# Decays a third phase ahead, and four pairs' x transposed by the DMA crossbar, in a fused recurrent-attention and MLP kernel

## Chip, cores, metric

One core of a Trainium2 chip. The metric is the device time of one execution in microseconds (us). A "run" below is one timed execution; every kernel has several, and the kernel before was timed beside each group of kernels on the same chip.

## The reference

Gated linear attention over 4 batches, 8 heads, 768 steps, heads of 48; its result, 3072 tokens of 384, goes through a GELU MLP of width 2048.

```python
for t in range(S):
    state = alpha[:, :, t, :, None] * state + einsum('bhd,bhe->bhde', k[:, :, t], v[:, :, t])
    y[:, :, t] = einsum('bhd,bhde->bhe', q[:, :, t], state)
x = y.transpose(0, 2, 1, 3).reshape(B * S, H * D)      # B, H, S, D = 4, 8, 768, 48
h = x @ w_in
g = 0.5 * h * (1 + tanh(sqrt(2 / pi) * (h + 0.044715 * h**3)))
out = g @ w_out
```

## The kernel before

Time is cut into 6 chunks of 128 steps; a **pair** is one chunk of two batches, so there are 12 pairs, 0 to 11. For each pair:

- the *decays*: `la` = ln(alpha) on ScalarE, its cumulative sum `cum` on TensorE, then `b`, `binv` and `bend` (exponentials) on ScalarE; VectorE makes `qp` = q·b and `kp` = k·binv;
- the transposes of qp and kp to `qkT`, by TensorE (through PSUM and a copy) or, for pairs 8 to 11, by the DMA crossbar;
- attention: `at` (scores), mask to `atm`, `kv` and the state, `y`;
- `x` is copied from `y` and transposed to `xT`: in this kernel always by TensorE through PSUM.

Each pair's tokens are then one **block** of the MLP: layer 1 (`hT`, 48 matmuls), GELU on ScalarE (`gT`), layer 2 (`acc`, 32 matmuls). A phase below is layer 1 and layer 2 of one block; the attention of later pairs is placed between these matmuls. ScalarE needs one table for ln and exp and another for GELU, so decays are done in stretches between the GELUs of two blocks:

```python
DECAYS = {-1: (0, 1), 1: (2, 3), 2: (4,), 3: (5,), 4: (6,), 5: (7,), 6: (8,), 7: (9,), 8: (10,), 9: (11,)}
TURN_QK, TURN_X = (8, 9, 10, 11), ()       # pairs whose qk, whose x go by the crossbar
```

Key 6 with value (8,) says: pair 8's decays come after block 6's GELUs. The rest is placed by a list scheduler that runs while the program is built, with an estimated duration for each task; it decides the order on every engine, and which of two engines does a copy. The two ways of transposing x, and what joins them:

```python
def turn_x_dma(self, u, i, c, b):
    return lambda e: self.nc.sync.dma_start_transpose(self.xT[c][:, :, b, :], u["x", i])
...
if m in self.TURN_X:
    xe = tx = s.add("turn", {"SP": W["turn"]}, P + 22 + j, self.turn_x_dma(u, j, c, b), [xc], xbar=W["xbar_x"])
else:
    tx = s.add("tx", {"PE": W["tx"]}, P + 22 + j, self.turn_x(u, j), [xc])
    xe = s.add("xe", {"DVE": W["xe"]}, P + 22 + j, self.turned_x(u, j, c, b), [tx])
```

All crossbar transposes and all stores of results are issued by SyncE, in one order. The loads of q, k, v and alpha are issued by GpSimd, but for the first of alpha.

Of the kernel before, what the change touches and what calls it, by code (L numbers as in the profile page):

```python
# [24 lines left out]
class Task:  # L25


    def __init__(self, kind, cost, prio, emit, deps=(), table=None, land=None, stream=None, xbar=0):
        self.kind, self.cost, self.prio, self.emit = kind, cost, prio, emit
        self.deps, self.takes = list(deps), []  # L30
        self.table, self.land, self.stream, self.xbar = table, land, stream, xbar
        self.end = self.done = None

    def take(self, tag, *users):
# [4 lines left out]
class Scheduler:  # L39
# [9 lines left out]
    def order(self):  # L49
        free = {e: 0 for e in LAT}  # L50
        taken = {tag: [] for tag in self.bufs}
        table, wire, xbar, head, out = LN_EXP, 0, 0, 0, []
        left = {e: sorted((t for t in self.tasks if e in t.cost), key=lambda t: t.prio) for e in LAT}

        def given(tag):

            n, at = len(taken[tag]) - self.bufs[tag], 0
            for u in taken[tag][n] if n >= 0 else ():
                if u.done is None:
                    return None  # L60
                at = max(at, u.done)
            return at

        def ready(t):
            if t.stream not in (None, head):
                return None
            at = 0
            for d in t.deps:
                if d.done is None:
                    return None  # L70
                at = max(at, d.done)
            for tag, _ in t.takes:
                g = given(tag)
                if g is None:
                    return None
                at = max(at, g)
            return at

        def put(t, at, e):
            nonlocal wire, xbar  # L80
            for tag, users in t.takes:
                taken[tag].append(users)
            t.start, t.end, t.engine, t.load = at, at + t.cost[e], e, None
            free[e] = t.end
            t.done = t.end + LAT[e]
            if t.land is not None:
                wire = t.done = max(wire, t.end + W["dma"] - t.land) + t.land
            if t.kind in ("turn", "store"):
                xbar = t.done = max(xbar, t.end + W["landed"] - t.xbar) + t.xbar
            out.append(t)  # L90

        while any(left.values()):
            best = None
            for e in LAT:
                found = []
                for t in left[e]:
                    at = ready(t)
                    if at is not None:
                        turn = W["table"] if t.table not in (None, table) else 0
                        at = max(at, free[e] + turn)  # L100
                        found.append((at, t, at - turn))
                if found:
                    window = min(f[2] for f in found) + 60
                    at, t, _ = min((f for f in found if f[2] <= window), key=lambda f: (f[1].prio, f[0]))
                    if best is None or at < best[0]:
                        best = at, e, t
            assert best is not None, "no task can go on"
            at, e, t = best
            if e == "PE" and self.fill and at < self.until and at - free[e] > 500:
                g = given("ff")  # L110
                n = int((at - max(free[e], g if g is not None else at) - 100) * 0.8 // W["fill"])
                if not free[e]:
                    n = int((at - W["zero"]) // W["cold"])
                if n > 0:
                    f = Task("fill", {"PE": n * W["fill"]}, 0, self.fill(n))
                    put(f.take("ff", f), max(free[e], g), e)
            put(t, at, e)
            if t.stream is not None:
                head += 1
            if t.table not in (None, table):  # L120
                table = t.load = t.table
            for q in t.cost:
                left[q].remove(t)
        return out
# [9 lines left out]
class _Kernel:  # L134

    BLOCKS = ((0,), (1,), (2,), (3,), (4,), (5,), (6,), (7,), (8,), (9,), (10,), (11,))
    DECAYS = {-1: (0, 1), 1: (2, 3), 2: (4,), 3: (5,), 4: (6,), 5: (7,), 6: (8,), 7: (9,), 8: (10,), 9: (11,)}

    SPLIT = (2,)
    EARLY = (0, 1)  # L140
    LOADS = ("0", "1", "in 0", "in 1", "in 2", "in 3", "out 0", "out 1", "out 2", "out 3",
             "2", "3", "4", "5", "6", "7", "8", "9", "10", "11")

    TURN_QK, TURN_X = (8, 9, 10, 11), ()
    BUFS = dict(ca=1, yk=2, ff=4, la=3, qp=3, kp=3, b8=2, qkT=3, atm=6, x=3, ot=6, bend=6,
                a=4, q=4, k=4, v=6)

    def __init__(self, ctx, tc, q, k, v, alpha, w_in, w_out, out):
# [24 lines left out]
                      for b in range(B)]  # L173
        self.ring = {n: [const.tile([C, 2, H, 64], F16 if n == "la" else BF16, name=f"{n}{i}")
                         for i in range(self.BUFS[n])] for n in ("la", "qp", "kp")}
        self.used = {n: 0 for n in self.ring}
# [5 lines left out]
    def tile(self, tag, shape, dt, name=None):  # L182
        pool = self.ps if tag in ("ca", "yk", "ff") else self.sb
        return pool.tile(shape, dt, tag=tag, bufs=self.BUFS[tag], name=name or tag)

# [73 lines left out]
    def exp(self, u, n, lo, hi):  # L259
        D, H = self.D, self.H  # L260

        def emit(e):
# [4 lines left out]
            else:  # L267
                if n not in u:
                    u[n] = self.sb.tile([self.C, 2, H, D], BF16, tag=n, bufs=self.BUFS["b8"], name=n)
                self.nc.scalar.activation(u[n].rearrange("t i h d -> t i (h d)")[:, lo:hi],  # L270
# [156 lines left out]
    def tasks(self):  # L427
        s = self.s = Scheduler(self.BUFS, self.fill, 60000)
        B, NCH = self.B, self.NCH
# [115 lines left out]
        f, gs, l2s = {}, {}, {}  # L545
        between = {m: [x for p in self.DECAYS.get(m, ()) for x in ends[p]] for m in range(-1, len(self.BLOCKS))}

# [15 lines left out]
        def layer2(m):  # L563
            nonlocal n
            units = [(pairs[p][0], 2 * pairs[p][1] + j) for p in self.BLOCKS[m] for j in range(2)]
            parts = range(self.NFT // 4)
            first = {}
            for u, part in ([(u, part) for part in parts for u in units] if m == 0 else [(u, part) for u in units for part in parts]):
                c, b = u
                t = s.add("l2", {"PE": W["l2"]}, 10000 + n, self.layer2(f, c, b, part),  # L570
                          gs[m][4 * part:4 * part + 4] + [loads["w", "out", part]], stream=n)
                l2s.setdefault(c, []).append(t)
                n += 1
                first.setdefault(u, t)
                if part == parts[-1]:
                    ot = s.add("ot", {"DVE": W["ot"], "ACT": W["ot_act"]}, -1, self.result(f, c, b), [t])
                    first[u].take("ff", ot)
                    ot.take("ot", s.add("store", {"SP": W["sp"]}, n, self.store(f, c, b), [ot]))

        for m in range(len(self.BLOCKS)):  # L580
            layer1(m)
            if m:
                for j in (0, 1) if m == 1 else (m,):
                    layer2(j)
        for m, ps in self.DECAYS.items():
            for p in ps if m >= 0 else ():
# [3 lines left out]
    def run(self):  # L590
# [5 lines left out]
        first = [lambda: make_upper_triangular(nc, self.ut_h, val=1.0, diag=True), lambda: make_identity(nc, self.ident)]  # L596
        for i in range(max(self.BUFS[n] for n in self.ring)):
            for n in self.ring:
                if i < self.BUFS[n]:
                    nc.vector.memset(self.ring[n][i][:, :, :, self.D:64], 0.0)  # L600
# [42 lines left out]
```

## Time and profile before

| | |
|---|---|
| time, median of 3 (range) | 190.5 us (190.08 to 190.57) |
| span of the profiled run; its time | 188.2 us; 190.31 us |
| TensorE, VectorE, ScalarE busy | 94%, 58%, 71% |
| table loads on ScalarE | 20 of 1.28 us |
| start of the last `ot` copy (the end of all matmuls) | 184.53 us |

How long the crossbar took for q and k, from the view of the tile qkT (time of the issue on SyncE, min/median/max in ns, start of the first and the last in us; then the time from issue to landing, of q and k together):

```profile
L308 SPq DMA_TRANSPOSE qkT<-kp x4: 1260/1294/1337, 122.0 to 162.0; - x4
DMA to landing us min/median/max: 3.1/3.2/5.0
```

Most land 3.2 us after issue.

### The profile page before, as it was taken

The numbers are of one execution on the slowest core, as the hardware profiler recorded it, in microseconds if no ns is written. First come the engines' busy times: TensorE is split into PE (matmuls) and PEld (weight loads), VectorE is DVE, ScalarE is ACT, GpSimd is POOL, SyncE is SP. The second block draws the span as 40 slices with busy tenths as digits, with TensorE's granted clock in tenths as the row PEclk, the third lists the DMA queues.
The fourth block names the chain that finished last, engine by engine and source line by source line (L and its number), as shares of the span: only waits on it lengthen the run. The fifth ranks groups of instructions, "written<-read, shape, count | busy, mean of one in ns | idle before, by whom it ended". The sixth has DMA issues, their size and how long they took to land.

```text
span 188.2 us, 4536 instructions
## 1 busy us (share of the span) xinstructions
PE 177.0 (94%) x1858; PEld 127.4 (68%) x1858; DVE 109.6 (58%) x231; ACT 133.1 (71%) x293; POOL 63.7 (34%) x67
## 2 busy tenths in 40 slices
PE   5778899999999999999999999989999999999992
PEld 1344688556687787787787787667686776876860
DVE  7388640179687596596596587555975627442000
ACT  2635889743869769769769769878698698662921
POOL 7993443795555566565510510000000000000000
PEclk9999999999999999999999999999999999999999
DMA  6999999999999999999999790290350430701101
GB/s 128 179 182 171 203 203 219 190 184 232 239 217 183 150 236 199 175 243 186 181 231 199 172 213 4 64 134 0 74 125 3 109 86 3 168 27 45 44 20 63
DMA packets 46452, 26.76 MB, mean 142 GB/s; under 512 B 36416, under 2 KB 43072, under 8 KB 46432
## 3 DMA queue, kind: packets, MB, share of 16 engines
q0 software_dynamic: 32464, 19.27, 73.4%
q1 hardware_dynamic: 13968, 7.21, 16.1%
q8 instruction: 14, 0.23, 0.5%
q14 instruction: 6, 0.05, 0.1%
HBM read 25.17 MB, written 4.72 MB: 159 GB/s over the span
## 4 chain that ended last, share of the span: by engine, by line
PE 72%; DMA 16%; POOL 6%; ACT 1%; issue 1%; DVE 1%; POOLq 0%; DVEq 0%
PE acc L412 29%; PE hT L398 26%; DMA w_out<-in_moe_w_out_dram 8%; DMA a<-in_alpha_dram 6%; PE at L325 4%; PE qkT_ps L289 3%; DMA qkT<-kp 2%; PE yps L371 2%; PE yps L374 2%; PE cum L252 2%; PE xT_ps L388 2%; POOL w_in L228 2%; PE kv L342 1%; POOL q L220 1%; POOL v L220 1%
## 5 line engine op out<-in xcount | busy, mean ns | idle before, releaser
L404 ACT ACTIVATE gT<-hT 128x256 bf16<-128x256 f32 x192 | 64.5, 384 | 17.7 <-PE hT L398 17.1
L398 PE MATMUL hT<-xT,w_in 128*128 128x256 bf16 x576 | 69.9, 273 | 0.4 <-DMA w_in<-in_moe_w_in_dram 0.2
L412 PE MATMUL acc<-w_out,gT 128*128 128x384 bf16 x384 | 69.4, 326 | 0.0
L398 PEld LDWEIGHTS <-w_in 128*128 128x128 bf16 x576 | 54.1, 98 | 9.0 <-DMA w_in<-in_moe_w_in_dram 0.6
L412 PEld LDWEIGHTS <-gT 128*128 128x128 bf16 x384 | 35.8, 98 | 19.5
L332 DVE TENSOR_TENSOR atm<-at,ut 128x512 bf16<-128x512 f32 x48 | 30.9, 686 | 17.4 <-PE at L325 16.3
L278 DVE TENSOR_TENSOR qp<-q,b 128x768 bf16<-128x768 f32 (+1 forms) x13 | 11.6, 893 | 23.9 <-ACT b L270 23.8
L220 POOL DMA_DIRECT2D a<-in_alpha_dram x12 | 13.3, 1107 | 16.8 <-ACT la L241 8.8
L220 POOL DMA_DIRECT2D q<-in_q_dram x13 | 14.6, 1120 | 10.4 <-DVE qp L278 3.3
L419 ACT COPY ot<-acc 128x384 f32<-128x384 f32 x13 | 6.2, 477 | 15.5 <-PE acc L412 15.5
L220 POOL DMA_DIRECT2D v<-in_v_dram x13 | 14.4, 1110 | 7.8 <-PE hT L398 1.8
L220 POOL DMA_DIRECT2D k<-in_k_dram x13 | 14.4, 1111 | 7.2 <-DVE kp L278 2.3
L241 ACT ACTIVATE la<-a 128x768 f16<-128x768 f32 (+1 forms) x13 | 10.3, 794 | 5.7 <-DMA a<-in_alpha_dram 5.6
L270 ACT ACTIVATE b<-cum 128x768 bf16<-128x768 f32 (+1 forms) x13 | 9.9, 761 | 5.2 <-PE cum L254 4.9
L198 ACT ACT_TABLE_LOAD x10 | 12.8, 1283 | 0.9 <-PEq L627 0.7
L381 DVE CAST x<-yps 128x384 bf16<-128x384 f32 x14 | 7.8, 556 | 9.3 <-PE yps L374 9.3
L404 ACT ACT_TABLE_LOAD x10 | 12.8, 1283 | 0.2
L359 DVE TENSOR_TENSOR st<-stmp,bend 64x192 bf16<-64x192 f32 x32 | 11.3, 353 | 2.1 <-ACT gT L404 0.5
L278 DVE TENSOR_TENSOR kp<-k,binv 128x768 bf16<-128x768 f32 (+1 forms) x15 | 11.7, 793 | 0.7 <-DMA k<-in_k_dram 0.7
L357 DVE TENSOR_TENSOR stmp<-kv,st 64x192 f32<-64x192 f32 x32 | 11.3, 352 | 0.3
L207 PE MATMUL idle<-zero 128*128 128x512 bf16 x34 | 10.2, 423 | 1.2 <-DVE zero L594 1.2
L325 PE MATMUL at<-qkT 64*128 64x128 bf16 x192 | 9.5, 219 | 1.3 <-DMA qkT<-kp 0.8
(43 smaller groups left out, 156.1 us busy)
## 6 DMA issues: line engine op xcount, KB each, us to landing
out_dram<-ot SPq DMA_DIRECT2D x24, 192.0 KB, 3.9
q<-in_q_dram POOLq DMA_DIRECT2D x11, 384.0 KB, 13.0
k<-in_k_dram POOLq DMA_DIRECT2D x11, 384.0 KB, 13.0
a<-in_alpha_dram POOLq DMA_DIRECT2D x10, 384.0 KB, 13.0
v<-in_v_dram POOLq DMA_DIRECT2D x11, 192.0 KB, 12.9
w_in<-in_moe_w_in_dram POOLq DMA_DIRECT2D x4, 384.0 KB, 11.9
w_out<-in_moe_w_out_dram POOLq DMA_DIRECT2D x4, 384.0 KB, 15.0
a<-in_alpha_dram SPq DMA_DIRECT2D x1, 384.0 KB, 4.0
```

The lines of the kernel that those rows point to most:

```text
L198: nc.scalar.add_instruction(mybir.InstLoadActFuncSet(name=nc.get_next_instruction_name(), act_func_set_id=i, engine=mybir.EngineType.Activ ...
L207: self.nc.tensor.matmul(ps, self.zero[:, 0:self.C], self.zero, start=True, stop=True)
L220: (nc.sync if e == "SP" else nc.gpsimd).dma_start(u[n][:, lo:hi].rearrange("t b h d -> t (b h) d"), src)
L241: self.nc.scalar.activation(u["la"][:, lo:hi, :, 0:self.D], u["a"][:, lo:hi], AF.Ln)
L278: self.nc.vector.tensor_tensor(u[n + "p"][:, lo:hi, :, 0:self.D], u[n][:, lo:hi], u["b" if n == "q" else "binv"][:, lo:hi], op=ALU.mult)
L325: nc.tensor.matmul(at[:, o, p, :], t[sl, 1, p, :], t[sl, 0, p, :], start=True, stop=True)
L332: self.nc.vector.tensor_tensor(u["atm", i][:, o], u["at", i][:, o], self.ut[:, None, :].to_broadcast([self.C, self.H // 2, self.C]), op=AL ...
L357: nc.vector.tensor_tensor(s[ps], acc, old[ps, :, fs], op=ALU.add)
L359: nc.vector.tensor_tensor(new[ps, :, fs], acc, u["bend"][ps, i, :, None].to_broadcast([64, H // 2, D]), op=ALU.mult)
L398: self.nc.tensor.matmul(h, self.w_in[:, j, nt * self.C:(nt + 1) * self.C], self.xT[c][:, j, lo:hi].rearrange("p g t -> p (g t)"), start=j ...
L404: return lambda e: self.nc.scalar.activation(self.gT[c % self.NG][:, nt, lo * self.C:hi * self.C], f.pop(("h", c, lo, nt)), AF.Gelu_apprx_ ...
L412: self.nc.tensor.matmul(f["acc", c, b], self.gT[c % self.NG][:, nt, b * self.C:(b + 1) * self.C], self.w_out[:, nt, :], start=nt == 0, sto ...
```

## The change

Its intent: give every decay, and so every transpose, one phase more before it is needed, and use that slack to take the last four pairs' x transposes away from TensorE too. The whole diff, without a field that it adds to the scheduler and leaves at zero:

```diff
-    DECAYS = {-1: (0, 1), 1: (2, 3), 2: (4,), 3: (5,), 4: (6,), 5: (7,), 6: (8,), 7: (9,), 8: (10,), 9: (11,)}
+    DECAYS = {-1: (0, 1), 1: (2, 3), 2: (4,), 3: (5,), 4: (6, 7), 5: (8,), 6: (9,), 7: (10,), 8: (11,)}
-    TURN_QK, TURN_X = (8, 9, 10, 11), ()
-    BUFS = dict(ca=1, yk=2, ff=4, la=3, qp=3, kp=3, b8=2, qkT=3, atm=6, x=3, ot=6, bend=6, ...)
+    TURN_QK, TURN_X = (8, 9, 10, 11), (8, 9, 10, 11)
+    BUFS = dict(ca=1, yk=2, ff=4, la=3, qp=4, kp=4, b8=2, qkT=4, atm=6, x=3, ot=6, bend=8, ...)
```

More of the change, by code (lines that the diff above doesn't have):

```diff
@@ L25, with __init__ @@
 class Task:
-    def __init__(self, kind, cost, prio, emit, deps=(), table=None, land=None, stream=None, xbar=0):
+    def __init__(self, kind, cost, prio, emit, deps=(), table=None, land=None, stream=None, xbar=0, late=0):
         self.kind, self.cost, self.prio, self.emit = kind, cost, prio, emit
@@ L31, in __init__ @@
         self.table, self.land, self.stream, self.xbar = table, land, stream, xbar
+        self.late = late
         self.end = self.done = None
@@ L89, in put @@
                 xbar = t.done = max(xbar, t.end + W["landed"] - t.xbar) + t.xbar
+                t.done += t.late
             out.append(t)
@@ L142 @@
              "2", "3", "4", "5", "6", "7", "8", "9", "10", "11")
-    TURN_QK, TURN_X = (8, 9, 10, 11), ()
-    BUFS = dict(ca=1, yk=2, ff=4, la=3, qp=3, kp=3, b8=2, qkT=3, atm=6, x=3, ot=6, bend=6,
+    TURN_QK, TURN_X = (8, 9, 10, 11), (8, 9, 10, 11)
+    BUFS = dict(ca=1, yk=2, ff=4, la=3, qp=4, kp=4, b8=2, qkT=4, atm=6, x=3, ot=6, bend=8,
                 a=4, q=4, k=4, v=6)
```

## The prediction

> **What bounds the kernel now.** I read the busy table first, then the windows over five stretches, then the chain that ended last, then the timeline of the one place where the chain leaves TensorE. Of the page I take one line, the busy time of each engine:
>
> ```profile
> PE 177.0 (94%) x1858; PEld 127.4 (68%) x1858; DVE 109.6 (58%) x231; ACT 133.1 (71%) x293; POOL 63.7 (34%) x67
> ```
>
> A share of 94% could still be the pipelined look of matmuls. So I take the windows: length, then the busy time of PE, PEld, DVE, ACT and POOL in each stretch.
>
> ```profile
> 40.00:60.00 20.00, 19.61 (x234) 14.02 (x233) 16.00 (x34) 13.27 (x31) 12.60 (x12) 1.00 1.30 217
> 60.00:101.00 41.00, 41.00 (x462) 31.08 (x460) 29.96 (x60) 32.47 (x71) 20.93 (x19) 1.00 1.52 201
> 101.00:115.00 14.00, 14.00 (x161) 10.64 (x160) 9.81 (x20) 11.15 (x25) 3.45 (x3) 1.00 0.73 163
> 115.00:131.00 16.00, 15.21 (x159) 10.90 (x158) 9.55 (x20) 13.25 (x26) 0.00 (x0) 1.00 0.33 58
> 131.00:171.00 40.00, 40.00 (x435) 29.50 (x433) 23.56 (x44) 29.91 (x66) 0.00 (x0) 1.00 0.30 70
> 171.00:185.00 14.00, 13.49 (x101) 9.57 (x99) 0.39 (x2) 7.05 (x20) 0.00 (x0) 1.00 0.12 43
> ```
>
> From 60 to 184 us TensorE has no gap except 0.79 us in 115 to 131 (16.00 less 15.21); the 0.5 us missing in the last row is the kernel's end, when only the last copy and store are left. All the other idle PE time (188.2 less 177.0, less 0.79, less the end) lies before 60 us, where the change moves nothing. The clock is 1.00 throughout. In the chain, the gap is this piece, columns start, length, what (it is TensorE itself on either side):
>
> ```profile
> 118.38 0.18 PE cum L252
> ...
> 120.40 0.95 DVE kp L278
> 121.35 0.51 DVE ot L419
> 122.00 4.29 DMA qkT<-kp
> 126.33 0.40 PE at L325 x8
> ...
> 132.64 0.17 PE xT_ps L388 x3
> ```
>
> The eighth index (pair 8) is the first whose q and k are transposed by the crossbar. Its k leaves at 122.00 and lands 4.29 us later, and TensorE, which had filled the time with layer 1, sat idle for the last 0.79 us of it. For pairs 9 to 11 the same transposes land in time: there is no gap from 131 on. The last line shown is what three x transposes cost in TensorE's stream: 0.17 us. So the kernel is a stream of matmuls in which, inside the part changed, only instructions taken out of the stream and that 0.79 us are worth anything.
>
> **What the Trainium skill says.** "Perfetto Trace Analysis", section Identifying the Most-Contended Engine: matmul busy time is no good measure of closeness to roofline, because matmuls are pipelined. The trace agrees: one x transpose has a record of 219 ns, while three together advance the chain by 0.17 us, so 57 ns each. I use the 57. "VectorE: DVE Perf Modes", section The three transpose paths: TensorE 390 ns against 1309 ns for the crossbar for 128x128 of bf16, with TensorE's result in PSUM. The latencies in the trace differ (219 ns; 3.1 to 5.0 us from issue to landing for the larger q and k tiles), but the direction is the same: the crossbar is longer in latency and takes nothing from TensorE or VectorE. "DMA: Bandwidth & Descriptors", section Rules for kernel authors: issue a DMA early and wait late, so that its fixed cost overlaps. This is the change's whole idea; the 4.29 us piece above is where the kernel before does it too late. "ScalarE: Activation LUTs", section What ACT_TABLE_LOAD costs: about 1283 ns, plus a drain of about 1380 ns. The trace has 20 loads of 1283 ns; no extra drain is seen, since la starts 1.29 us after the load does.
>
> **The change part by part.** I compared the instruction order of the two kernels on each engine. Up to the decays after layer 1 of block 4 (about 104 us in the trace of before) they agree.
>
> *x by crossbar, pairs 8 to 11.* Each pair has two x tiles, so 8 tiles. TensorE loses 24 transposes (1858 matmuls become 1834): 8 x 0.17 = **1.36 us off the path**. VectorE loses 8 copies of xT at 352 ns, 2.8 us, and the PSUM pool yk 8 turns; neither bounds a stretch. Two more buffers each filled once with zeros (qp and kp, 165 ns each) come at the start, while VectorE waits for the first b. SyncE gains 8 transposes of 1.3 us issue each at most (the q and k ones measure 1293 ns) in a queue that mostly waits: beside. The landing, about 3.2 us, would hurt if layer 1 of the same block followed at once. In the new order it doesn't: pair 11's last y stands before the last 20 matmuls of block 9's layer 2, and layer 1 and layer 2 of block 10 (80 matmuls, 5.2 + 5.2 us at the chain's 109 and 163 ns each) come before x of pair 11 is needed. Worth of the landing: 0.
>
> *Decays three phases ahead.* Pairs 6 and 7 are taken together after block 4, each later one a phase earlier. Two table loads go (9 of each kind in place of 10), 2 x 1.28 = 2.6 us of ScalarE, off the path. The q and k transposes of pairs 9 to 11 get several us more; pair 8's are used not about 4 but by my count about 3.5 us after the k issue (see below). If they land in time, **0.79 us** comes off the path.
>
> *The price, in the phases of blocks 5 to 7.* The double decay puts one more la (0.84), b, binv (0.81 each) and bend (0.18) before block 5's first gelu, 2.6 us as records, about 2.2 as they pipeline. Before, that gelu came at 107.47 (for this block; the b activation starts at 104.5). After, I walk it: b, binv, bend of pair 6 from 104.5 to 106.1; the second cum stands 12 acc matmuls (1.96 us) after the first, so at 106.5 to 106.8; pair 7's three to 108.4; table load to 109.7. TensorE meanwhile has 4 acc, 16 qkT transposes (0.89), two layer-1 tiles, at and kv, to about 109.7, and four PSUM buffers of ff hold what comes. So it just fits: 0 to 0.5 us of stall. VectorE must do four pairs' attention in about three phases: two pairs with copies (2 x 10.6 us: 1.9 for qp and kp, 2.7 masks, 1.4 qkT copies, 2.8 state, 1.1 x, 0.7 xT) and two without (2 x 8.5), with three or so ot copies, about 40 us in 43, where it had 10 us of 14 before. Walking the order I find two tight places: the mask of pair 7's second tile against its y (0 to 0.3 us) and pair 8's k transpose against its first at (kp ends near 128.0, landing near 131.3, at near 131.5: 0 to 0.8 us). I take **0.5 us** back for all of these.
>
> Sum: 190.5 - 1.36 - 0.79 + 0.5 = 188.85, so 188.8 us. The 2.1 us between span and time stay as they are.
>
> **The rivals.** *A new wait takes the place of the old one.* ScalarE or VectorE falls behind in blocks 5 to 7 and TensorE stands still by 1 to 3 us there. For it: the 92% of VectorE that I count, and the double decay. Against: the same ordering rule placed these instructions, and it left no gap on VectorE's or ScalarE's account from 60 us on before. Time: 190 to 191. *The crossbar's queue becomes the bound*: 8 transposes more on one queue, with stores and the wait of each for its x; one late piece holds all that follow. Against: each is needed a phase later, some 10 us against 3 to 5. Time if pair 8's landing is late as before: 189.6. *Everything fits, and regularity pays more*: no stall, and the 0.1 to 0.2 us by which a phase exceeds the sum of its pieces (I sum 13.95 for a phase of 14.15) shrink: 188.0. *A large gain*, over 2%, would need 3.8 us; the gaps and the instructions removed are worth 2.15 together, so only something the profile doesn't show could give it.
>
> **Range and chances.** Both gains in full and nothing back: 188.35, a little less with the third rival, so the low end is 187.8. The high end is the first rival at its middle, 190.2. Runs of before spread by 0.5 us. Faster by over 2% (below 186.7): 4%. Slower by over 2% (above 194.3): 2%. Within: 94%.
>
> **What would show it.** In the profile after: 1834 matmuls on TensorE; 18 table loads; VectorE's busy time near 107.1 (109.6 less 2.8, plus the two fills) and ScalarE's near 130.5; no xT_ps group after pair 7; the piece DMA qkT<-kp gone from the chain, and no x transpose in its place; TensorE full from block 7 to the end. The stall term is right if the idle PE time between 104 and 145 us sums to 0 to 1 us. I would be wrong if that sum is 2 us or more (then the name behind it, ACT or DVE, tells which rival), if an at or a layer 1 waits for a crossbar transfer, or if the transposes taken out leave gaps in their place.

## The result

188.73 us, median of 4 runs (188.62 to 189.1), against 190.51 us. Ratios in this document are the mean time of one kernel's runs over that of the other's of the same rounds, so not quite the ratio of the medians: 0.9915, 95% interval 0.9895 to 0.9935. Executions over 1.5% slower than the fastest of the same kernel are left out of the means. Within 2%, faster by about 0.9%, and 0.07 us from the predicted time.

The busy line after, then the two windows that answer to those of before (columns as in the prediction; the last three are the granted clock, the mean busy share of a DMA engine, and GB/s moved):

```profile
PE 176.7 (95%) x1831; PEld 127.2 (68%) x1834; DVE 104.0 (56%) x219; ACT 131.8 (71%) x297; POOL 63.8 (34%) x67
```

```profile
115.00:131.00 16.00, 15.82 (x184) 11.53 (x182) 12.09 (x26) 13.27 (x31) 0.00 (x0) 1.00 0.40 87
131.00:171.00 40.00, 40.00 (x381) 29.06 (x378) 13.27 (x21) 28.32 (x66) 0.00 (x0) 1.00 0.30 72
```

TensorE's weight loads are 1834, as counted (three matmul records are missing). From 60 to 171 us TensorE lacks 0.18 us, where before it lacked 0.79. In the chain, no transfer of this part is left; the one piece that isn't TensorE's is ScalarE's:

```profile
121.07 1.97 PE acc L414 x12
...
123.06 0.48 ACT ot L421
...
123.56 1.28 ACT L406
...
124.85 0.39 ACT gT L406
...
125.29 1.14 PE hT L400 x9
```

A copy of a result and the table load delay block 7's first GELU, and layer 1, with all four of its PSUM buffers full, waits 0.17 us. The crossbar's landings, in the views of the tiles qkT and xT:

```profile
L310 SPq DMA_TRANSPOSE qkT<-kp x4: 1232/1288/1295, 113.7 to 150.4; - x4
DMA to landing us min/median/max: 3.0/3.2/3.4
L316 SPq DMA_TRANSPOSE xT<-x x8: 1178/1184/1212, 121.7 to 159.2; - x8
DMA to landing us min/median/max: 2.3/2.3/2.4
```

Pair 8's k now goes out at 113.7 and not 122.0, and none takes over 3.4 us. Its first reader in TensorE's timeline:

```profile
117.72 0.40 PE L327 MATMUL at<-qkT 64*128 64x128 bf16 x8
```

**Who got the third phase's slack.** Not q and k. From the issue of a pair's k to the moment when TensorE came to its first `at`, pairs 8 to 11 had 3.54, 3.23, 3.85 and 3.84 us before, and have 4.00, 3.18, 3.61 and 3.25 after; k lands 0.96, 0.12, 0.44 and 0.13 us ahead of that moment. It is x that got the slack: it has landed 7.3 to 13.6 us before its layer 1. So pair 8's wait went for two reasons: its k had 0.46 us more, and it landed 1.25 us sooner (3.04 us for 4.29). With the old landing some 0.3 us of wait would be left, by estimate (4.29 + 0.05 from landing to start - 4.00).

**Where the 1.8 us lie.** I use three marks of the trace: the start of layer 1 of block 2 (everything before it is the same order), the start of the last `ot` copy, and the end of the span. The *path* is the time from the first mark to the second; the *tail* is the time from the end of that copy (its start plus 0.48) to the end of the span.

| | block 2's layer 1 | last copy | path | tail | span | time less span |
|---|---|---|---|---|---|---|
| before | 50.32 | 184.53 | 134.21 | 3.19 | 188.2 | 2.1 |
| after | 50.28 | 182.76 | 132.48 | 3.66 | 186.9 | 1.8 |

The path is 1.73 us shorter. Of that, x transposes give 1.38 (in TensorE's stream their slots add up to 2.05 us from 90 us on before and 0.67 after), the wait 0.79; 0.17 comes back as the GELU wait and about 0.27 in no named wait. The tail is 0.47 us longer, and the part of the time outside the span 0.3 us shorter. These two were not in the prediction, and nearly cancel. (Spans are printed to 0.1 us, so a tail is good to 0.05 us.)

### The profile page after: what moved, and what is told of

Same layout as the page of the kernel before. It is cut to its first block, busy times and chain, and to the rows that moved or that the text cites. A ratio compares the mean times of both kernels' runs of the same rounds, so it can differ in the third digit from the quotient of the medians.

```text
span 186.9 us, 4504 instructions
## 1 busy us (share of the span) xinstructions
PE 176.7 (95%) x1831; PEld 127.2 (68%) x1834; DVE 104.0 (56%) x219; ACT 131.8 (71%) x297; POOL 63.8 (34%) x67
## 4 chain that ended last, share of the span: by engine, by line
PE 88%; ACT 4%; DVE 3%; DMA 2%; issue 1%
PE hT L400 34%; PE acc L414 34%; PE at L327 4%; PE qkT_ps L291 4%; PE cum L254 3%; PE yps L376 2%; DMA a<-in_alpha_dram 2%; PE yps L373 2%; PE kv L344 2%; PE idle L209 2%; PE xT_ps L390 1%; DVE atm L334 1%; ACT qkT L305 1%; PE cum L256 1%; DVE qp L280 1%
## 5 line engine op out<-in xcount | busy, mean ns | idle before, releaser
L406 ACT ACTIVATE gT<-hT 128x256 bf16<-128x256 f32 x192 | 63.5, 386 | 11.0 <-PE hT L400 10.5
L414 PE MATMUL acc<-w_out,gT 128*128 128x384 bf16 x384 | 68.6, 326 | 0.0
L334 DVE TENSOR_TENSOR atm<-at,ut 128x512 bf16<-128x512 f32 x48 | 31.0, 686 | 13.8 <-PE at L327 12.9
L421 ACT COPY ot<-acc 128x384 f32<-128x384 f32 x17 | 8.2, 480 | 18.7 <-PE acc L414 18.5
L209 PE MATMUL idle<-zero 128*128 128x512 bf16 x31 | 11.2, 483 | 1.4 <-DVE zero L596 1.2
L200 ACT ACT_TABLE_LOAD x9 | 11.5, 1283 | 0.9 <-PEq L629 0.7
L406 ACT ACT_TABLE_LOAD x9 | 11.5, 1283 | 0.2
L305 DVE COPY qkT<-qkT_ps 128x1024 bf16<-128x1024 bf16 (+1 forms) x14 | 8.8, 649 | 4.7 <-PE qkT_ps L291 4.6
L383 DVE CAST x<-yps 128x384 bf16<-128x384 f32 x12 | 6.7, 556 | 7.6 <-PE yps L376 7.5
```

The source lines that it names most:

```text
L200: nc.scalar.add_instruction(mybir.InstLoadActFuncSet(name=nc.get_next_instruction_name(), act_func_set_id=i, engine=mybir.EngineType.Activ ...
L209: self.nc.tensor.matmul(ps, self.zero[:, 0:self.C], self.zero, start=True, stop=True)
L305: self.copy(e)(t, u.pop(("T_ps", i, which)))
L334: self.nc.vector.tensor_tensor(u["atm", i][:, o], u["at", i][:, o], self.ut[:, None, :].to_broadcast([self.C, self.H // 2, self.C]), op=AL ...
L406: return lambda e: self.nc.scalar.activation(self.gT[c % self.NG][:, nt, lo * self.C:hi * self.C], f.pop(("h", c, lo, nt)), AF.Gelu_apprx_ ...
L414: self.nc.tensor.matmul(f["acc", c, b], self.gT[c % self.NG][:, nt, b * self.C:(b + 1) * self.C], self.w_out[:, nt, :], start=nt == 0, sto ...
```

## The experiments

Twelve kernels, all of them timed in five rounds. All gave correct results but the last. The table has all of them; "wait" is the sum of the waits of 0.17 us and more that TensorE shows from 84 us on. Path, tail and wait are of the profiled run alone; x_from_six and x_from_four spread by more than the rest (194.68 to 198.17 and 202.83 to 205.61 us; profiled: 197.37 and 202.83).

| kernel | time (us) | ratio to before | path | tail | wait |
|---|---|---|---|---|---|
| before | 190.28 to 190.54 (medians) | 1 | 134.21 | 3.19 | 0.79 |
| after | 188.73 | 0.9915 | 132.48 | 3.66 | 0.17 |
| 1 x_alone | 192.58 | 1.0120 | 136.40 | 3.65 | 3.57 |
| 2 decays_alone | 190.03 | 0.9984 | 133.88 | 3.18 | 0.17 |
| 3 pair8_tensor | 189.61 | 0.9966 | 134.21 | 2.85 | 0 |
| 4 double_late | 190.60 | 1.0022 | 134.44 | 3.68 | 2.14 |
| 5 x_last_two | 188.88 | 0.9918 | 133.18 | 3.07 | 0.17 |
| 6 x_from_six | 195.78 | 1.0255 | 141.89 | 2.99 | 7.97 |
| 7 qk_from_seven | 202.26 | 1.0620 | 146.59 | 3.12 | 13.21 |
| 8 x_from_four | 204.16 | 1.0731 | 147.06 | 3.26 | 11.45 |
| 9 stores_split | 188.00 | 0.9871 | 132.47 | 3.02 | 0.18 |
| 10 double_seven | 188.60 | 0.9897 | 132.34 | 3.66 | 0.37 |
| 11 old_buffers | 188.81 | 0.9909 | 132.47 | 3.64 | 0.18 |
| 12 qk_from_seven_few | 187.91 | 0.9876 | 132.32 | 3.11 | 1.00 |

The theory from the result: x transposes are worth their slots in TensorE's stream, the longer lead is worth the wait of pair 8, and each works alone. The rivals: the crossbar is only hidden because of the third phase (so the parts don't add), or one of the parts carries everything.

### 1 and 2: one part alone

x_alone is the kernel before with

```diff
-    TURN_QK, TURN_X = (8, 9, 10, 11), ()
+    TURN_QK, TURN_X = (8, 9, 10, 11), (8, 9, 10, 11)
```

> The kernel before with x of pairs 8 to 11 by the crossbar, decays left two phases ahead. My theory: 24 transposes leave TensorE (8 x 0.17 = 1.36 us), the wait of pair 8's first at for its k (0.79 us) stays, and the new order puts 20 to 28 layer-2 matmuls (3.3 to 4.6 us) between the last y and the layer 1 that needs it, against about 0.56 + 2.3 us for copy and landing: 189.1 us (188.9 to 189.5), no hT waiting for an x transfer by over 0.3 us. Rival A, the crossbar's landing is exposed without the third phase: 0.5 to 1.5 us for each of four pairs, 190.5 or more. Rival B, the gain is all in the decays: 190.5.

decays_alone is the changed kernel with

```diff
-    TURN_QK, TURN_X = (8, 9, 10, 11), (8, 9, 10, 11)
+    TURN_QK, TURN_X = (8, 9, 10, 11), ()
```

> The changed kernel with x transposed by TensorE throughout. My theory: only the 0.79 us wait goes, less the 0.2 us of new stall seen in the changed kernel: 189.9 us (189.6 to 190.2), and TensorE idle in the middle under 0.4 us. Rival A, the longer lead carries the whole gain: 188.9. Rival B, the double decay costs as much as it saves: 190.5.

My expectation for x_alone was wrong by 3.5 us: it is slower than the kernel before by 1.2%, as rival A had it. TensorE's timeline of x_alone, the lines with a wait (in brackets: length, and what ended it):

```profile
126.52 0.40 PE L325 MATMUL at<-qkT 64*128 64x128 bf16 x8 [0.84 <-DMA qkT<-kp]
135.88 1.48 PE L398 MATMUL hT<-xT,w_in 128*128 128x256 bf16 x12 [0.27 <-DMA xT<-x]
137.87 1.47 PE L398 MATMUL hT<-xT,w_in 128*128 128x256 bf16 x12 [0.51 <-ACT gT L404]
139.87 0.40 PE L325 MATMUL at<-qkT 64*128 64x128 bf16 x8 [0.53 <-DMA qkT<-kp]
163.07 1.49 PE L398 MATMUL hT<-xT,w_in 128*128 128x256 bf16 x12 [0.56 <-DMA xT<-x]
164.78 1.80 PE L398 MATMUL hT<-xT,w_in 128*128 128x256 bf16 x15 [0.22 <-ACT gT L404]
167.22 0.40 PE L325 MATMUL at<-qkT 64*128 64x128 bf16 x8 [0.64 <-DMA qkT<-kp]
```

Two kinds of wait are new. Layer 1 waits for xT of pairs 8 and 10: x lands in 2.3 to 4.3 us here, where my sum had 2.3. That two halves share one queue is not the reason: the second halves went out 0.02 us after their copies had ended, and pair 9's, sent the same way, landed in 2.3 us with no wait. And `at` of pairs 9 and 11 waits for k: the queue issues in order, so their q and k stand behind the x of the pair before, whose second half took 2.0 us to issue in place of 1.2. That is the queue's rival of my prediction, and here it is real.

What the slow transfers have in common stands in the DMA view. A packet of 16 KB on a queue of the kind "instruction" (a fetch of instructions) starts at 133.0, 160.6 and 173.0 us, amid the x transfers of pairs 8, 10 and 11; five of these six halves took 3.1 to 4.3 us, and the sixth had all but landed. The view of the DMA queues of x_alone from 133 to 134.3 us (packets, MB, share of the 16 DMA engines):

```profile
q1 hardware_dynamic: 374, 0.09, 32.8%
q8 instruction: 1, 0.02, 5.8%
```

The 5.8% are 1.2 us of one engine's time. Pair 8's q and k meet such a fetch too, here (123.7 us) and in the kernel before (123.6 us). I counted all fourteen traces, transposes issued after the last load, "slow" being over 3.5 us for q and k and over 2.75 us for x: of 26 with a fetch between issue and landing 18 are slow; of 166 without, 2 are, each right behind a slow one. None of the changed kernel's 16 meets a fetch. No experiment moved a fetch, so this is a strong link and not a proof. If it is the cause, x_alone doesn't tell what x by crossbar costs without the third phase: landing in the usual 2.3 us, x of pairs 8 and 10 would have been there 0.7 and 0.3 us before layer 1 came, and the queue would have been free for q and k 0.8 us sooner, more than the 0.53 and 0.64 us that `at` waited (estimates from this trace).

decays_alone gains 0.16%. Its path is 0.33 us shorter than before, not the 0.6 I expected: the 0.79 us wait is gone, 0.17 came back, and some 0.3 us is in no named wait, as in the changed kernel. From decays_alone to the changed kernel the path falls from 133.88 to 132.48, 1.40 us: 8 x 0.17 = 1.36 was the slots' worth. So x by crossbar costs 2.2 us of path when it stands alone and gives 1.4 when the decays are ahead. The parts don't add: the decays make room for x's transfers. How much of the 2.2 us is owed to the fetches, no run tells.

### 3 and 4: is pair 8's wait the transfer, and where must the double decay lie?

pair8_tensor is the kernel before with `TURN_QK` = (9, 10, 11).

> The kernel before with q and k of pair 8 transposed by TensorE and not by the crossbar. If the gap of 0.79 us is the late landing of pair 8's k, it disappears and 16 transposes (16 x 56 ns = 0.89 us) take its place: 190.6 us (190.3 to 190.9), and no gap over 0.2 us from 60 us to the end. Rival: the gap is owed to the decays' own chain (b, qp, kp on ScalarE and VectorE) and not to the transfer; then it stays at 0.5 us or more and the time is 191.2 or more.

No gap is left from 60 us to the end, and the path is 134.21 us, as before to the digit: the 0.79 us wait was the transfer's, and 16 transposes on TensorE cost what it cost (0.89 us by my estimate). Whether the transfer was late for its short lead or for the fetch beside it, this run can't tell. The time is 0.67 us lower than before all the same, against my 190.6 (190.3 to 190.9): a miss. The trace puts it outside the path: the tail is 0.34 us shorter, and the time less the span is 1.8 us in all five runs, where the kernel before had mostly 2.0 to 2.3.

double_late is the changed kernel with

```diff
-    ... 4: (6, 7), 5: (8,), 6: (9,), 7: (10,), 8: (11,)}
+    ... 4: (6,), 5: (7,), 6: (8, 9), 7: (10,), 8: (11,)}
```

> The changed kernel with the double decay put at pairs 8 and 9 (after block 6), so pair 8 has no longer a lead than before; x by crossbar for pairs 8 to 11. My theory: what matters is pair 8's lead; TensorE's order now has only about 5.8 us of work between pair 8's decays and its first at, where before it had 7.0 and waited 0.8 more, so it waits 0.8 to 1.9 us there: 189.2 to 190.3 us. Rival: only the number of table loads and of decay stretches matters, and where the double one lies is indifferent: 188.7.

190.6 us, a little beyond the range that my theory gave, and 1.9 above the changed kernel, so the place matters. TensorE's lines with a wait:

```profile
124.27 1.14 PE L400 MATMUL hT<-xT,w_in 128*128 128x256 bf16 x9 [1.04 <-ACT gT L406]
125.77 0.40 PE L327 MATMUL at<-qkT 64*128 64x128 bf16 x8 [0.36 <-DMA qkT<-kp]
137.89 1.48 PE L400 MATMUL hT<-xT,w_in 128*128 128x256 bf16 x12 [0.29 <-DMA xT<-x]
143.15 0.40 PE L327 MATMUL at<-qkT 64*128 64x128 bf16 x8 [0.45 <-DMA qkT<-kp]
```

The larger wait is not pair 8's k but GELU. As I read it, two pairs' exponentials in one stretch hold ScalarE longer, and here TensorE has no qk transposes to do meanwhile, since pair 8's go by crossbar. In the changed kernel pair 6's 16 transposes (0.89 us) stand in that place. This is a size that my theory left out. The other three waits go with fetches, at 121.3 and 135.5 us.

### 5 to 8: how far does it carry?

Each is the changed kernel with other pairs in `TURN_X` or `TURN_QK`: x for (10, 11); x from 6; q and k from 7; x from 4.

> The changed kernel with x by crossbar for pairs 10 and 11 only; pairs 8 and 9 by TensorE. A dose: 12 transposes come back, 4 x 0.17 = 0.68 us on the path. My theory (with three phases of lead each x transpose moved is worth just its slots in TensorE's stream): last copy 0.7 us later than in the changed kernel, 189.3 us (189.0 to 189.6). Rival (what pays is less traffic on one queue or in PSUM's yk buffers, not the slots): a change of under 0.2 or over 1.2 us.

> The changed kernel with x by crossbar for pairs 6 and 7 too, at about 98 to 115 us, while the loads still run. My theory: 12 transposes fewer, 0.68 us, since the new order has some 6 us of other work between pair 6's last y and the layer 1 that needs it, against 0.6 + 2.3 to 4.3 us: 188.0 us (187.7 to 188.4). Rival: beside the loads the crossbar's landing goes to 6 us and more, and a layer 1 waits for xT by 0.5 us or more: 188.7 or later.

> The changed kernel with q and k of pair 7 by crossbar too, issued near 95 to 98 us. My theory: 16 transposes fewer on TensorE, 16 x 56 ns = 0.89 us, and a lead of some 8 us (pair 7 is decayed with pair 6, a phase early) that covers a landing of 3 to 6 us: 187.9 us (187.6 to 188.4). Rival: the landing beside the loads is longer than the lead, at of pair 7 waits for kp by over 0.5 us: 188.7 or later.

> The changed kernel with x by crossbar from pair 4 on. Pairs 4 and 5 have a lead of two phases only, so x is needed by the layer 1 that follows within 3 to 5 us, and the loads are in flight. Theory from the run with x alone: the transfers of pairs 4 and 5 are exposed, 0.3 to 1.5 us each, so it is later than x from pair 6 by 0 to 2 us: 188.3 to 190. Rival (the lead doesn't matter): 187.3.

x_last_two is the dose that the theory wants: path 133.18, 0.70 us above the changed kernel, for 0.68 expected. Its time, 188.88 us, lies below my range all the same: it rises by 0.15 us only, as its tail is 0.59 us shorter (experiment 9). By the time alone the rival (under 0.2 us) would have won; only the path tells them apart.

The other three are far slower than I expected. For x_from_six and qk_from_seven the rivals had said so; x_from_four is 14 us beyond its range, and its rival (187.3) was wrong too. In qk_from_seven TensorE stands still for 12 us, before the first `at` of pair 7:

```profile
104.44 2.11 PE L414 MATMUL acc<-w_out,gT 128*128 128x384 bf16 x12
118.61 0.61 PE L327 MATMUL at<-qkT 64*128 64x128 bf16 x8 [12.06 <-DMA qkT<-kp]
```

The view of qkT says that of its ten transposes the median lands in 3.2 us and the longest in 21.9. In x_from_six one x took 13.8 us and layer 1 waited 7.4 us; in x_from_four layer 1 of blocks 4 and 5 waited 5.8 and 3.9 us. A long wait is also paid twice: in x_from_six the 15 layer-1 matmuls after it took 3.38 us, where such 15 take 1.80, and the granted clock was 0.55 in that stretch of 10 us. These transfers are issued from about 71 to 104 us, beside the loads. That suggests the loads; experiment 12 tests it for qk_from_seven, and for the other two it stays untested.

### 12: is it the loads?

qk_from_seven once more, with TensorE's order unchanged, but pairs 9 to 11 read the tensors of pair 8, so their loads fall away (and results are wrong); the part of the diff that does it:

```diff
+            if 2 * c + i >= 8:
+                u[n] = self.shared[n]
+                if 2 * c + i > 8:
+                    return
```

> The run with q and k of pair 7 by crossbar, its TensorE order unchanged, but pairs 9 to 11 read pair 8's q, k, v and alpha (wrong results on purpose), so the last load is issued near 80 us and lands before the transposes at 96 us. Theory: the 21.9 us of landing were the loads' doing; without them pair 7's q and k land in 3.0 to 3.5 us, the wait of 12 us goes, and the time is what the removed slots promise: 187.9 us (187.4 to 188.3). Rival: the crossbar queue itself, or its order behind stores and other transposes, makes them late; then the landing stays over 8 us and the time over 195.

187.91 us, as expected, but partly by luck: the path is only 0.16 us shorter than the changed kernel's, where 0.89 was due, as `at` of pair 11 waits 0.82 us (a fetch at 145.1 us falls on pair 10's x, and the queue is behind); the tail, shorter by 0.55 us, makes up for it. Windows of qk_from_seven and then of this kernel, the same stretch; the last column is what the DMA engines moved, in GB/s:

```profile
95.00:100.00 5.00, 5.00 (x70) 4.23 (x67) 4.89 (x11) 4.61 (x14) 2.31 (x2) 1.00 1.49 239
100.00:105.00 5.00, 5.00 (x62) 3.80 (x61) 4.16 (x11) 4.18 (x8) 1.15 (x1) 1.00 1.13 183
110.00:115.00 5.00, 0.00 (x0) 0.00 (x0) 0.00 (x0) 0.00 (x0) 0.00 (x0) 0.50 1.33 125
```

```profile
95.00:100.00 5.00, 5.00 (x70) 4.23 (x66) 4.89 (x11) 4.61 (x14) 0.00 (x0) 1.00 0.37 83
100.00:105.00 5.00, 5.00 (x62) 3.80 (x61) 4.15 (x11) 4.18 (x8) 0.00 (x0) 1.00 0.28 54
110.00:115.00 5.00, 5.00 (x67) 4.57 (x64) 4.08 (x10) 4.35 (x13) 0.00 (x0) 1.00 0.75 141
```

The transposes go out at the same times (96.1 and 102.4 us), and the longest landing is 3.4 us in place of 21.9. With that the cause of the 12 us is shown: a crossbar transfer issued beside the loads. How the loads hold it up (by packets, by the memory, or by the order within the DMA engines) no run here tells.

### 10 and 11: which lead, which buffers?

double_seven doubles pairs 7 and 8: `5: (7, 8), 6: (9,), ...`. Pair 8 keeps its three phases, but its transposes fall beside the last loads.

> The changed kernel with the double decay at pairs 7 and 8 (after block 5): pair 8 has the same three phases of lead, but its transposes go out about 107 to 109 us, and pair 7 keeps two, so the loads of pairs 9 to 11 run later, to about 120 us. Theory 1, loads decide: beside the loads the crossbar lands in 5 to 15 us, pair 8's first at (some 5 us after its k) waits 1 us or more: 190 to 196. Theory 2, the lead decides: as good as the changed kernel, 188.5 to 189.2.

Theory 1 was wrong in its size: the longest landing, 6.0 us, is twice the usual, but no `at` waits for a transfer; 188.6 us and a path of 132.34 are as good as the changed kernel's. From q's issue to its `at` there are 10.4 us here, which cover a landing of 6.0; qk_from_seven had 10.5, which don't cover 21.9.

old_buffers has the buffer counts of before in the changed kernel.

> The changed kernel with the buffers of before (qp, kp and qkT 3 each in place of 4, bend 6 in place of 8). TensorE's order differs in one place only (a cum stands four matmuls later or so). Theory: the added buffers are not what pays: 188.5 to 189.1, as the changed kernel. Rival: without them qp or kp of pair 9 wait for pair 6's readers, and TensorE idles 0.5 us or more.

188.81 us: the added buffers do nothing here.

### 9: the tail

> The changed kernel with the first four stores cut into two halves each, which only adds instructions to SyncE (99 in place of 92). In the four runs with 92 SyncE instructions a transfer of about 8 KB appears 3.0 to 3.25 us after the last copy, and the span ends 3.65 to 3.68 us after it; in the runs with 72, 76, 84, 96 and 100 it doesn't, and the end comes 2.85 to 3.2 us after it. Theory: that transfer is a fetch of instructions that 92 happens to put at the very end; here it is gone, the last copy stays at 182.8 us of the span, and the span ends 0.4 to 0.6 us sooner: 188.2 us (188.0 to 188.5). Rival: the longer end comes with the number of transposes or transfers on that queue; then no gain: 188.7.

The edit, to the function that stores a result, of chunk 0 only:

```diff
-        return lambda e: self.nc.sync.dma_start(self.out[r:r + self.C, :], f["ot", c, b])
+            n = 2 if c == 0 else 1
+            for i in range(n):
+                p, q = i * self.C // n, (i + 1) * self.C // n
+                self.nc.sync.dma_start(self.out[r + p:r + q, :], f["ot", c, b][p:q])
```

Windows after the last copy, of the changed kernel and then of this one; in the second line the last store moves, the third is what follows to the end:

```profile
183.99:184.74 0.75, 0.00 (x0) 0.00 (x0) 0.00 (x0) 0.00 (x0) 0.00 (x0) 1.00 0.72 262
184.74:186.85 2.11, 0.00 (x0) 0.00 (x0) 0.00 (x0) 0.00 (x0) 0.00 (x0) 1.00 0.01 4
```

```profile
183.93:184.68 0.75, 0.00 (x0) 0.00 (x0) 0.00 (x0) 0.00 (x0) 0.00 (x0) 1.00 0.72 262
184.68:186.10 1.42, 0.00 (x0) 0.00 (x0) 0.00 (x0) 0.00 (x0) 0.00 (x0) 1.00 0.00 0
```

The store itself moves in the same window after the copy. In the changed kernel something small follows at the very end (4 GB/s over 2.11 us is about 8 KB; the view of the DMA queues from 186 us on shows one packet, on a queue of the kind "instruction"), here not, and the tail is 3.02 us in place of 3.66, with the same path. The five kernels whose SyncE program has 92 instructions (after, 1, 4, 10, 11) have tails of 3.64 to 3.68; those with 72 to 84 or 96 to 108 have 2.85 to 3.26. In those five such a packet starts 0.3 to 0.6 us before the end of the span; in this kernel the last one starts at 174.2 us. Adding seven instructions took the longer tail away, with as many transposes and four stores more, so the rival (the number of transposes or transfers) is out, and the length of SyncE's program is shown to decide it. That the end waits for this fetch is inferred. **188.00 us is the fastest correct version here**, a ratio of 0.9871, and beats both kernels.

## Why the prediction was right

- **x transposes, 1.36 us.** Right: 1.38 us of slots in the trace, 1.40 from decays_alone to the changed kernel, 0.70 for half of them.
- **"Worth of the landing: 0".** Right in the changed kernel, by the reason given, the third phase: x has landed 7.3 us or more before its layer 1. Without it the same transfers cost 2.2 us of path, the fetches of experiment 1 included.
- **The wait of 0.79 us.** Right: it disappeared, and pair8_tensor shows that it was the transfer's. But the several us more of lead that it counted on for pairs 9 to 11 did not come (their k got none), and pair 8's k got 0.46 us. That all four were in time is in part luck: pair 8's transfers took 3.4 us at most where they had taken 4.3 and 5.0, and pairs 9 and 11 have 0.12 and 0.13 us in hand. It was not the loads that made them slow before, for the DMA engines moved next to nothing from 113 to 119 us; a fetch of instructions fell on them (experiment 1). Against the queue's rival, too, the prediction said that each transfer is needed some 10 us after its issue: that is true of x, and not of k (3.2 to 4.0 us).
- **The price, 0.5 us.** 0.17 us in a named wait, about 0.27 us unnamed. The walk through the double decay predicted the first GELU 5.2 us after `b`; it came after 5.4 (90.34 to 95.71) with no stall. Pair 8's k was seen as tight, with 0 to 0.8 us of wait; it landed 1.0 us ahead of its `at`. The 0.17 us lies in a place that I had not looked at, block 7's first GELU.
- **An error that cost nothing, by luck.** The text puts the parting of the two orders at about 104 us. That is block 5's layer 2; block 4's is at 90 us, as the trace after shows. I had counted the layer-1 blocks one too late. All intervals were taken between neighbours, so they held. But pair 8's q and k went out at 111.7 and 113.7 us and not near 128, as the loads' last packets ran (to 112.3 us); in double_seven, where q went out at 110.5, it took 6.0 us to land.
- **What was not in the sum.** "The 2.1 us between span and time stay as they are" was wrong: they became 1.8. And the tail grew by 0.47 us. The path fell by 1.73 against a predicted 1.65; that the time came out at 188.73 for 188.8 is helped by these two nearly cancelling.
- **The signs.** 18 table loads, no xT by TensorE after pair 7, and no wait for a transfer: as said. TensorE is full from block 7 on, but for the 0.17 us. VectorE is busy 104.0 us and not 107.1, ScalarE 131.8 and not 130.5: the scheduler gave ScalarE four `ot` copies and two x copies more, which a count of removed instructions misses.

What stays open: the 0.27 us; whether the fetches cause the slow landings; and why the kernel before and decays_alone have mostly 2.0 to 2.3 us between span and time, and the other kernels 1.7 to 1.85. In the traces of these two, a packet of 8 KB on the queue q14 of the kind "instruction" starts 1.9 us after the end of the span; in x_last_two one starts 0.3 us after it, in the others none. That it makes the difference was not tested.

## What to carry to other kernels

A transfer that takes work off the bounding engine is worth just that work (here 1.40 us for slots of 1.36), if its landing and its place in an in-order queue are covered; ask how much lead it has before asking how much it saves, and test the lead and the transfer each alone. Measure the lead from the issue to the first reader: with decays a phase ahead x has 7 us and more in hand, and k at most 1. Where a transfer has only 0.1 to 1 us in hand, look for fetches of instructions in the DMA view. Look at what else moves on the DMA engines at the moment of issue: the same transposes landed within 3.4 us with the loads taken away, and in up to 21.9 beside them. When changes are under 1%, measure from one mark of the trace to another, since the end of a program has effects of its own of half a microsecond.

## What the Trainium skill lacked or had wrong

- "Advanced Engine Details and Errata", section X-Bar Transpose (TRN2), says that transpose DMAs are as fast as regular ones; "DMA: Bandwidth & Descriptors", section Rules for kernel authors, that a transpose next to ordinary DMAs needs nothing. For correctness the runs agree. For time both lack the latency under load: 3.0 to 3.4 us for these q and k tiles with the loads taken away, up to 21.9 us beside them, where the loads themselves take 13 us in the median.
- "VectorE: DVE Perf Modes", section The three transpose paths, compares single latencies (390 and 1309 ns). It lacks the cost in a stream, which is what decided here: 57 ns of TensorE's time for each 128x128 transpose.
- "ScalarE: Activation LUTs", section What ACT_TABLE_LOAD costs, adds about 1380 ns of drain to each 1283 ns load. The traces show 1283 ns, and the next activation 1.29 us after the load's start.
- "Runtime: NRT & Kernel Launch" has a section on the end of a program and one on the fetching of instructions. The first lacks that the end can depend on a program's length: a tail of 3.66 us where SyncE had 92 instructions, and 3.02 where it had 99. The second lacks what a fetch goes with on the DMA engines: of 26 crossbar transposes with one beside them 18 were slow, of 166 without 2.
